# Linear attention and a phase-mixing layer on one core: loading k and v in runs of 5 and 4 tokens, from two queues

## The chip, the core and the metric

One Trainium2 core runs the whole computation in one launch. Its engines each work off their own list of instructions in order: TensorE (matmuls, "PE", weight loads "PEld"), VectorE ("DVE"), ScalarE ("ACT"), GpSimd ("POOL") and SyncE ("SP", which here only issues transfers). Transfers (DMAs) are issued from SyncE, ScalarE and GpSimd, each with its own queue, and are carried by 16 DMA engines. The metric is device time in microseconds; three runs of the kernel before gave 206.93, 206.5 and 206.49 us, with a median of 206.5.

## What is computed

Batch 8, 8 heads of 64 columns, 576 tokens. Linear attention per head, an RMS norm, then a layer that turns each value by an angle and mixes tokens and channels:

```python
kv = np.einsum('bhsd,bhse->bhde', k, v)
out = np.einsum('bhsd,bhde->bhse', q, kv)
x = out / np.sqrt(np.mean(out * out, axis=-1, keepdims=True) + 1e-06) * g_norm   # then heads side by side
theta = x @ w_theta
y = einsum('ts,bsd->btd', w_tok_r, x * cos(theta)) + einsum('ts,bsd->btd', w_tok_i, x * sin(theta))
u = x + y
result = u + np.maximum(u @ w_ch, 0.0)
```

kv sums over all 576 tokens, so it does not matter which token lies on which partition, as long as k and v agree.

## The kernel before

Work is cut into tasks: loads, matmul groups, evacuations, stores. Each has an engine, or a choice of several, and the order in which all tasks are issued is a table of numbers, `TURNS`, played by `play`. A number is a task; a star behind it picks the second of its engines. Entries such as `r9` or `a7` stand for 9 or 7 matmuls of a tile of ones ("fill") with the identity that nobody reads (`idle`); `s2` and `p13` are gates (`hold`): SyncE or GpSimd waits there until the load of that number in the list `landed` has come in.

Per batch b the chain is: load k, v (`loads`), q; **kv** on TensorE (line 301, 4 head pairs, 80 matmuls a batch), copied to `kbd`; q turned by TensorE (line 316) or by a transposing DMA; **raw** = q kv (359); square on ScalarE (381), sums (390), root (GpSimd; for batch 0 ScalarE and VectorE), x (422); x turned to `xT`; **theta** (487) with `wth`; the angle as an integer (503, 509, 513, 519), sine and cosine on ScalarE (526), z (549); **y**, the token mix, with the turned token weights `wT` (572); u into `wn` (577); u turned; **v**, the channel mix (487 again, with `wch`); the sum into `ot` (619), stored (631, 635). The token weights are loaded by GpSimd (`wn`, `wnt`) and turned on TensorE at the start (648, 649); ScalarE changes its function table once from square roots to sines, in the head.

A k or v tile has 128 partitions. Partition p holds tokens 4p to 4p+3 of every head (`heads_in`, line 233: pieces of 1 KB); the last 64 tokens, the **tail**, lie in a column block of their own on partitions 0 to 63 (`tails_in`, line 239: pieces of 256 B), and the same block on partitions 64 to 127 is cleared once (`clear_tails`). kv is five matmul steps j per head: four for the heads' runs, the fifth for the tail. For batch 0 the k loads of either half of the heads are on SyncE's queue, the v loads on ScalarE's, both tails on SyncE's, and kv is split: all of `kvm` (j 0 to 3), then `kvt` (the tail). From batch 1 on, all loads of k and v are on SyncE's queue. Two buffers each (`NKV`) hold k and v, so a load waits for the kv two batches earlier.

Of the kernel before, what the change touches and what calls it, by code (L numbers as in the profile page):

```python
# [17 lines left out]
class Task:  # L18

    def __init__(self, name, engs, fn, deps, takes):  # L20
        self.name, self.engs, self.fn, self.deps, self.takes = name, engs, fn, deps, takes
        self.readers, self.unless = [], []
        self.other, self.at = False, None
# [6 lines left out]
    def run(self):  # L30
        if len(self.engs) == 1:
            self.fn()
        else:
            self.fn(self.engs[int(self.other)])
# [33 lines left out]
r3 a7 r7 r9 6 5 0 2 32 33 1 9 10 r1 a1 4 r2 38 39* 46 3 26 8 47 27 28 29 30 11 12 34 35 36 37 15 7  # L68
54 62 31* 40 41 55* 56 57 14 63* r5 42 43 13 70 71 58 59 44 45 s2 60 123 124* 16 48 49 127 17 72
128 64 65 73 61 50 81 82 66 74 51 52 67 79 80 p13 23 119 24 201 25 68 53 75 95 76 77 120* 89 87 19  # L70
78 200 131 96 69 88* 132* 90 91* 92 85 86 113 97 83 121 122* 21 114 115* 98 107 116 84 93 20 135
94 136* 199 99 100 101 102 103* 125 104 126 108 117 109* 110 129 118 145 137 105 106 111 112 130
22 153 133 18 134 202 203 204 205 206 344 222 154 198 207* 223* 208 138 139 140 146 147 209 210
211 165 224 225 236 215 212 166 237 226 167 229 216* 347 155 141 230 148 156 213 214 142 143 144
157 354 355 168 158 217 149 150 227 228 151 161 493 218 245 219 246* 243 244* 152 220 231 232 233
234 162 368 163 164 196 259 260 261 197 221 253 238 239 369* 235 174 175 240 195 169 170 262 176
254 247 255* 345 241 159 346 491 248 342 249 250 341 256 242 177 171 265 343 361 251 492 271 263
160 264 348 349 362 172 266 189 350 351 252 267* 268 190* 257 277 191 272 273* 258 269 270 274 179
180* 181 352 353 356 487 192 184 182 278 279 280 488 357 358 359 186 185 187 382 303 275 370 371
311 500 299 276 307 304 312 372 373 383 281 282 375 300 360 374 637 308 501 514 309 310 515 313  # L80
314 363 364 389 384 385 376* 494 495 390* 386 365 496 497 634 387 388 391 305 306 498 392* 377 378
379 499 399 400 301 366 367 302 507 508 401 402 380 397 398 381 283 284 502 503 405 188* 639 521
504 406 505 522 285 286 295 296 516 407 408 517 395 396 393 394* 489 173 287 288 289 490 518 506
325 178 646 519 330 290 403 404 409 331* 417 410 411 412 633 657 297 509 510 520 528 327 635 326
636 291 511 769 537 523 298 413* 414 292 293 418 529 419 524 525 420 538 512 513 294 335 336* 328
337 415 638 526 421 640 641 527 422 642 643 765 644 530 423 424 425* 645 535 536 338 551 332 541
647 426 427 416 539 333 428 329* 429 457 531 532 552 648 458 553 540* 542 545 649 546 547* 548 441
430 431 668 442 443 533 534 320 459 432 449 788 460 767 777 334 554 658 659 450 543 557 660 768
650 651 544 563 444 549 451 452 550 558 661 662 652 653 654 655 321 555 564 453 674 315 454 455
456 565 445 316* 559 663 664 556 446 447 448 317 665 656 569 570 764 318 771 481 482* 772 773 571  # L90
774 775 669 483 437 560 438 666 667 566 676 194* 433 434 572 439 319* 670 671 672 484 675* 776 435
# [12 lines left out]
611 840 749 841 842 843 756 940 942 1034 1035 1044 1045 1036 845 844 750 857 858 943 944 1046 1037
945 859 752 753 860 938 754 746 747 1049 861 941 873 757 1047 751* 1048 1060 946 947 966 967 968
846 847 1038 865 866 1050 849 850 851 862 969 951 848 1051 1052 970 1039 1054 939 971 863 864 952
867 868 852 869 870 954 874 955 956 875 953 1040 853 871 872 854 855 856 876 960 961 880 1061* 957
748 1041 1042 962 963 958 1072 1073 1053 1062 959 964 965 988 1055 1056 1057 1066 1067 883 884 885
989 881 877 878 1058 1059 1064 886 990 887 972 973 991 974 975 1004 1063* 1000 984 631* 985 1074*
882 980 981 986 1075 1076 632 1001 982 1002 888* 987 996 997 998 1078 1068* 1003 1065 1007 1077  # L110
983 1069 999 1006 976 992 993 1079 1070 1080* 1081 994 995 977 1082 978 979 1005 1083 1090 1091
1092* 1093 1020 891 1021 1022 1023 1071 889 890 879 1094 1095 1084 1085 1086 892 1087 1014 1008
893 762 1011 1009 763* 1010* 1017 1012 1015 894 1016 1116 1117 1100 1101 1018 1019 1013 1124 1125
1096 1088 1089 1102 1118 1119 1103 1126 1127 1097 1098 1099 1108 1109 1110 1111 1104 1105 1106
1107 1128 1129 1025* 1024* 1139 1112 1113 1114 1130 1131 1132* 1120 1140 1141 1115 1133 1142 1121
# [28 lines left out]
def kernel(  # L144
# [12 lines left out]
    nc = tc.nc  # L157
    B, H, S, D = q.shape
    C = H * D
    P = 128  # L160
# [807 lines left out]
```

## Time and profile before

| what | value |
|---|---|
| median of three runs | 206.5 us |
| the profiled execution | 206.64 us |
| its span, first to last instruction | 204.9 us |
| granted TensorE clock | 0.999 |
| HBM read, written | 33.06 MB, 9.44 MB |
| DMA queue of SyncE (q1) | 52788 packets, 29.17 MB |
| DMA queue of GpSimd (q0) | 15664 packets, 11.49 MB |
| DMA queue of ScalarE (q10) | 1056 packets, 1.05 MB |

The profile is one execution. Busy times overlap between engines; a busy TensorE is not TensorE at its peak, since matmuls are pipelined. A row of instructions names the line, the engine, the operation, and output<-inputs by the program's names; in brackets stands the idle time before it and what ended that. The chain of waits is followed back from the last instruction, at each step to what released it.

### The profile page before, as it was taken

The page shows a single profiled execution, that of the slowest core. Times are in us where ns is not written, and L with a number is a line of the kernel's source. Part 1 is how long each engine was busy: PE and PEld are TensorE (multiplying, and loading weights), DVE is VectorE, ACT ScalarE, POOL GpSimd, SP SyncE. Part 2 cuts the span into 40 slices and gives each one's busy share as a digit, 9 for nine tenths or more (in the row PEclk, how much of TensorE's full clock was granted, in tenths as well). Part 3 has the DMA queues.
Part 4 walks back from the last instruction along what each step waited for, and adds up shares of the span by engine and source line. Part 5 has one row for each costly group of instructions (what it writes and reads, how often), then busy time and mean ns, then how long its engine had stood idle before and what let it go on. Part 6 is the DMA issues. An engine that isn't in the chain of part 4 may idle for free.

```text
span 204.9 us, 5367 instructions
## 1 busy us (share of the span) xinstructions
PE 194.6 (95%) x2137; PEld 136.3 (67%) x2137; DVE 174.8 (85%) x366; ACT 128.3 (63%) x236; POOL 93.2 (45%) x99
## 2 busy tenths in 40 slices
PE   7997798999999999999999999999999999999990
PEld 2475567875778778666866686766866746766850
DVE  6038998898998799999999998998999989897661
ACT  2046998539992989949689678863666670572020
POOL 8310190479146778285673383365664335003013
PEclk9999999999999999999999999999999999999999
DMA  5999999999999999999998929699994545564415
GB/s 189 274 209 202 256 315 188 211 293 297 259 251 233 232 269 258 258 176 180 247 231 253 212 16 241 170 291 287 223 195 128 141 118 146 149 89 141 144 52 182
DMA packets 69532, 42.05 MB, mean 205 GB/s; under 512 B 39828, under 2 KB 65876, under 8 KB 69508
## 3 DMA queue, kind: packets, MB, share of 16 engines
q1 hardware_dynamic: 52788, 29.17, 60.4%
q0 software_dynamic: 15664, 11.49, 33.6%
q10 hardware_dynamic: 1056, 1.05, 1.5%
q8 instruction: 17, 0.28, 0.5%
q14 instruction: 7, 0.06, 0.1%
HBM read 33.06 MB, written 9.44 MB: 207 GB/s over the span
## 4 chain that ended last, share of the span: by engine, by line
PE 69%; DMA 13%; DVE 7%; ACT 5%; issue 2%; SPq 2%; POOL 0%; POOLq 0%; DVEq 0%; ACTq 0%
PE acc L572 29%; PE acc L487 22%; DMA kt<-in_k_dram 13%; PE acc L301 7%; PE tr L316 4%; PE acc L490 3%; PE raw L359 3%; DVE arg L519 2%; DVE x L422 1%; ACT kbd L321 1%; ACT sqb L381 1%; DVE ss L390 1%; SPq L233 1%; ACT arg L509 1%; ACT arg L503 1%
## 5 line engine op out<-in xcount | busy, mean ns | idle before, releaser
L572 PE MATMUL acc<-wT,zm 128*128 128x320 f16 (+1 forms) x512 | 76.7, 286 | 0.0
L400 POOL TENSOR_TENSOR rt<-ss,mhalf 128x8 f32<-128x8 f32 x28 | 47.9, 1714 | 48.1 <-DVE ss L390 48.1
L572 PEld LDWEIGHTS <-zm 128*128 128x128 f16 x512 | 48.2, 98 | 14.7 <-issue 0.9
L526 ACT ACTIVATE sc<-arg 128x1024 f16<-128x1024 int32 x32 | 33.9, 1064 | 10.7 <-DVE arg L519 10.6
L577 DVE SCALAR_TENSOR_TENSOR wn<-acc,gcol,xT 128x320 f16<-128x320 f32 (+1 forms) x64 | 31.4, 510 | 4.8 <-PE acc L572 4.4
L487 PE MATMUL acc<-wth,xT 128*128 128x512 f16 x128 | 31.9, 379 | 0.0
L487 PE MATMUL acc<-wch,wn 128*128 128x512 f16 x128 | 31.8, 379 | 0.1
L503 ACT ACTIVATE arg<-acc 128x512 int32<-128x512 f32 x32 | 19.0, 599 | 10.2 <-PE acc L487 5.0
L519 DVE TENSOR_SCALAR arg<-arg 128x1024 int32<-128x1024 int32 x32 | 23.3, 731 | 1.0 <-ACT arg L509 0.6
L390 DVE TENSOR_REDUCE ss<-sqb 128x8 f32<-128x520 f32 x32 | 21.8, 687 | 1.6 <-ACT sqb L381 1.5
L381 ACT ACTIVATE sqb<-raw 128x512 f32<-128x512 f32 x28 | 16.9, 603 | 8.9 <-PE raw L359 7.1
L301 PE MATMUL acc<-vt,kt 128*64 128x64 f32 x640 | 21.6, 223 | 0.9 <-DMA kt<-in_k_dram 0.9
L549 DVE TENSOR_TENSOR zm<-x,sc 128x1024 f16<-128x1024 f16 x32 | 21.6, 683 | 0.9 <-ACT sc L526 0.8
L301 PEld LDWEIGHTS acc<-vt,kt 128*64 128x64 f32 x640 | 20.3, 138 | 2.2 <-issue 1.8
L631 POOL DMA_DIRECT2D out_dram<-ot x14 | 8.3, 595 | 28.0 <-DVE ot L619 28.0
L422 DVE TENSOR_TENSOR x<-raw,rt 128x512 f16<-128x512 f32 x28 | 19.1, 684 | 1.2 <-POOL rt L400 0.8
L487 PEld LDWEIGHTS <-wn 128*128 128x128 f16 x128 | 12.0, 98 | 11.6 <-issue 0.6
L487 PEld LDWEIGHTS <-xT 128*128 128x128 f16 x128 | 11.8, 98 | 10.9 <-issue 0.2
L572 PE MATMUL acc<-wT,zt 128*128 128x320 f16 (+1 forms) x64 | 18.3, 286 | 0.0
L321 ACT COPY us<-tr 128x512 f16<-128x512 f16 x12 | 6.9, 587 | 13.0 <-PE tr L598 10.8
L400 POOL TENSOR_TENSOR rte<-sse,mhalf 128x4 f32<-128x4 f32 x7 | 9.0, 1284 | 13.0 <-DVE sse L390 13.0
L321 ACT CAST kbd<-acc 64x256 f16<-64x256 f32 (+1 forms) x32 | 11.1, 345 | 6.1 <-PE acc L301 5.6
(101 smaller groups left out, 275.0 us busy)
## 6 DMA issues: line engine op xcount, KB each, us to landing
vt<-in_v_dram SPq DMA_DIRECT2D x7, 1024.0 KB, 9.1
kt<-in_k_dram SPq DMA_DIRECT2D x7, 1024.0 KB, 11.5
out_dram<-ot SPq DMA_DIRECT2D x18, 256.0 KB, 3.2
qh<-in_q_dram POOLq DMA_DIRECT2D x7, 512.0 KB, 9.3
out_dram<-ot POOLq DMA_DIRECT2D x14, 256.0 KB, 3.8
kt<-in_k_dram SPq DMA_DIRECT2D x2, 512.0 KB, 4.7
vt<-in_v_dram ACTq DMA_DIRECT2D x2, 512.0 KB, 8.6
kt<-in_k_dram SPq DMA_DIRECT2D x8, 128.0 KB, 7.8
```

What stands on the lines that cost most here:

```text
L301: nc.tensor.matmul(t[i * D:(i + 1) * D, hp - lo, :], ks, vs, start=(hp == lo and j == 0), stop=(hp == lo + n - 1 and j == NT - 1),)
L321: nc.scalar.copy(out=dst, in_=src)
L390: nc.vector.reduce_sum(out=ss[:], in_=sq_sb.pop((b, j))[:], axis=AXX)
L400: nc.gpsimd.tensor_tensor(out=rt[:], in0=ss[:], in1=mhalf[:, 0:h], op=ALU.pow)
L422: nc.vector.tensor_tensor(out=x_pair[b, p][:, :, a * HC:(a + 1) * HC].rearrange("p t (h e) -> p h t e", e=D), in0=r[:].rearrange("p (h t e ...
L487: nc.tensor.matmul(t[:], piece(kc), w[:, kc, :], start=first, stop=last)
L503: nc.scalar.activation(out=arg[:, 0, :], in_=th_ps[b, j][:], func=AFT.Copy, scale=PER_TURN)
L519: nc.vector.tensor_scalar(out=arg[:], in0=arg[:], scalar1=32 - FINE, scalar2=None, op0=ALU.logical_shift_left)
L526: nc.scalar.activation(out=sc[:], in_=arg_sb.pop((b, j))[:], func=AFT.Sin, bias=0.0, scale=ANGLE,)
L549: nc.vector.tensor_tensor(out=dst, in0=x.unsqueeze(1).broadcast_to((P, 2, w)), in1=sc[:], op=ALU.mult)
L572: nc.tensor.matmul(t[:, 0:hi - lo], s, wT[:, w, lo:hi], start=n == 0, stop=n == len(z) - 1)
L577: nc.vector.scalar_tensor_tensor(out=uTb[b % NUT][:, c, lo:hi], in0=y_ps.pop((b, h, c))[:, 0:hi - lo], scalar=gcol[:, 0:1], in1=xTb[b % NX ...
```

## The change

Partition p of 0 to 63 now holds tokens 5p to 5p+4 (`fives_in`, pieces of 1280 B), partition 64+p holds tokens 320+4p to 320+4p+3 (`fours_in`, pieces of 1 KB). There are no tails; the fifth run's place on partitions 64 to 127 is cleared, now inside each head's columns. All `fives_in` are issued by SyncE, all `fours_in` by ScalarE, for every batch. kv of batch 0 is no longer split into main part and tail. Stores of the last batch may also go to ScalarE's queue (`+` in the table picks a task's third engine).

```diff
-    def heads_in(eng, dst, src, b, hs):
+    def heads_of(t):
+        return t[:].rearrange("p (h e) -> p h e", h=H)
+
+    def fives_in(eng, dst, src, b, hs):
         eng.dma_start(
-            out=rows_of(dst)[:, hs, :],
-            in_=src[b, hs, 0:SM, :].rearrange("h (p j) d -> p h (j d)", j=NJ),
+            out=heads_of(dst)[0:TL, hs, :],
+            in_=src[b, hs, 0:TL * NT, :].rearrange("h (p j) d -> p h (j d)", j=NT),
         )
-    def tails_in(eng, dst, src, b, hs):
+    def fours_in(eng, dst, src, b, hs):
         eng.dma_start(
-            out=tails_of(dst)[0:TL, hs, :],
-            in_=src[b, hs, SM:S, :].rearrange("h s d -> s h d"),
+            out=heads_of(dst)[TL:P, hs, 0:NJ * D],
+            in_=src[b, hs, TL * NT:S, :].rearrange("h (p j) d -> p h (j d)", j=NJ),
         )
...
-            nc.vector.memset(t[TL:P, H * NJ * D:H * NT * D], 0.0)
+            nc.vector.memset(heads_of(t)[TL:P, :, NJ * D:NT * D], 0.0)
...
+    def parts_in(n, t, src, b, hs, w, old):
+        return [add(f"load {n}{b}A{w}", "SP", lambda: fives_in(nc.sync, t, src, b, hs), old),
+                add(f"load {n}{b}B{w}", "ACT", lambda: fours_in(nc.scalar, t, src, b, hs), old)]
...
         for n, t, src in (("k", kt, k), ("v", vt, v)):
-            t = t[b % NKV]
-            k_ += [add(f"load {n}{b}", "SP",
-                       lambda t=t, src=src: heads_in(nc.sync, t, src, b, all8), old),
-                   add(f"load {n}{b}e", "SP",
-                       lambda t=t, src=src: tails_in(nc.sync, t, src, b, all8), old)]
+            k_ += parts_in(n, t[b % NKV], src, b, all8, "", old)
...
-            fin.readers = [add(f"st{w} {b} {j}{hh}", "SP|POOL",
+            fin.readers = [add(f"st{w} {b} {j}{hh}", "SP|POOL|ACT" if split else "SP|POOL",
...
-r3 a7 r7 r9 6 5 0 2 32 33 1 9 10 r1 a1 4 r2 38 39* 46 3 26 8 47 27 28 29 30 11 12 34 35 36 37 15 7
-54 62 31* 40 41 55* 56 57 14 63* r5 42 43 13 70 71 58 59 44 45 s2 60 123 124* 16 48 49 127 17 72
+r9 3 r8 r1 2 0 19 12 8 1 28 6 7 29 30* 31* a5 5 36 37 44 45* 4 32 33 46 34 35* 9 52 10 53* 60 38
+47 48 39 40 61 54 55 56 11 68 69 r3 41 42 43 49 62 63 16 21 57 58 17 117 118 121 122 50 59 70 71
+s10 13 14 125 126 64 65 77 78 72 51 73 76 66 22 74 75 129 79 80* 15 87 88 89 85 67 86* 23 93 130*
```

The whole table is new. The idle matmuls in it: before r3 a7 r7 r9, r1 a1 r2 and r5, 35 in all, 26 of them ahead of the first kv; now r9 r8 r1, a5 and r3, 26 in all, 18 ahead of the first kv. The gates: before, SyncE waits for batch 0's k tail (`s2`) and GpSimd for the tail of the real token weights (`p13`); now SyncE waits for the imaginary token weights (`s10`, `wn_86`) and GpSimd for the real ones (`p12`). The first list below is SyncE's order at the start of the program (kt_64 and vt_66 are batch 0's tiles, kt_65 and vt_67 batch 1's; sqe is the place of g_norm), before:

```order
L233 DMA kt_64<-in_k_dram 128x4x256 x2
L239 DMA kt_64<-in_k_dram 64x8x64
L275 DMA sqe_97<-in_g_norm_dram 1x64
L239 DMA vt_66<-in_v_dram 64x8x64
L676 DMA gate_100<-kt_64 1x1
L239 DMA kt_65<-in_k_dram 64x8x64
L239 DMA vt_67<-in_v_dram 64x8x64
L233 DMA vt_67<-in_v_dram 128x8x256
L233 DMA kt_65<-in_k_dram 128x8x256
```

and now:

```order
L230 DMA vt_66<-in_v_dram 64x4x320
L230 DMA kt_64<-in_k_dram 64x4x320
L272 DMA sqe_97<-in_g_norm_dram 1x64
L230 DMA vt_66<-in_v_dram 64x4x320
L230 DMA kt_64<-in_k_dram 64x4x320
L670 DMA gate_101<-wn_86 1x1
L230 DMA vt_67<-in_v_dram 64x8x320
L230 DMA kt_65<-in_k_dram 64x8x320
```

The tails are gone from both sides of the gate, and the gate reads another load. ScalarE's list in the head, between the first and the second change of its function table, before (sqb, sqe: squares; rs, rse: roots; wT: turned token weights; arg: angles):

```order
L381 ACTIVATE sqe_98<-acc_200 128x4x64
L455 ACTIVATE xT_82<-tr_194,gcol 128x4x128
L409 ACTIVATE rs_334<-ss_323 128x8
L409 ACTIVATE rs_338<-ss_330 128x8
L455 ACTIVATE xT_82<-tr_187,gcol 128x4x128
L409 ACTIVATE rse_359<-sse_332 128x4
L413 ACT_TABLE_LOAD
L413 ACTIVATE warm<-quarter 128x1
L503 ACTIVATE arg_384<-acc_182 128x512
```

and now:

```order
L403 ACTIVATE rs_329<-ss_327 128x8
L449 ACTIVATE xT_82<-tr_189,gcol 128x4x128
L403 ACTIVATE rse_340<-sse_336 128x4
L407 ACT_TABLE_LOAD
L407 ACTIVATE warm<-quarter 128x1
L497 ACTIVATE arg_365<-acc_182 128x512
L503 ACTIVATE arg_365<-acc_182 128x512
L236 DMA vt_67<-in_v_dram 64x8x256
L497 ACTIVATE arg_391<-acc_225 128x512
L497 ACTIVATE arge_399<-acc_155 128x256
```

A load of batch 1's v now stands between the angles of batch 0's theta; 17 more of its 18 loads stand elsewhere in ScalarE's list. In all, SyncE's loads of k, v and g_norm go from 33 to 19. The end of GpSimd's list held the last batch's stores, before:

```order
L635 DMA out_dram<-ote_1313 64x256
L631 DMA out_dram<-ot_755 128x512
L635 DMA out_dram<-ote_875 64x256 x2
L631 DMA out_dram<-ot_755 128x512
L631 DMA out_dram<-ot_881 128x512
L635 DMA out_dram<-ote_1313 64x256 x2
```

and now ScalarE's list ends with two of them, while GpSimd's ends with one `ote` store:

```order
L520 ACTIVATE sc_401<-arg_365 128x1024
L315 COPY us_703<-tr_196 128x512
L315 COPY us_705<-tr_189 128x512
L625 DMA out_dram<-ot_747 128x512
L629 DMA out_dram<-ote_1575 64x256
```

The last `ote` tile's two halves are stored from two queues, and the copy of the last turned u (`use`), the last thing ScalarE did before, is now VectorE's.

More of the change, by code (lines that the diff above doesn't have):

```diff
@@ L22, in __init__ @@
         self.readers, self.unless = [], []
-        self.other, self.at = False, None
+        self.other, self.at = 0, None
     def free_at(self):
@@ L33, in run @@
         else:
-            self.fn(self.engs[int(self.other)])
+            self.fn(self.engs[self.other])
 class Slots:
@@ L124, in play @@
     for turn in turns:
-        if turn.endswith("*"):
-            tasks[int(turn[:-1])].other = True
+        if turn[-1] in "*+":
+            tasks[int(turn[:-1])].other = "*+".index(turn[-1]) + 1
     for at, turn in enumerate(turns):
@@ L628, in store @@
         ot = ot_sb[b, j]
-        queue = nc.gpsimd if e == "POOL" else nc.sync
+        queue = {"SP": nc.sync, "POOL": nc.gpsimd, "ACT": nc.scalar}[e]
         if full(j):
@@ L693 @@
     got, q_got, k_got = {}, {}, {}
-    def halves_of_0(eng, e, t, src, n):
-        a = [add(f"load {n}0a", e, lambda: heads_in(eng, t, src, 0, lo4)),
-             add(f"load {n}0e", "SP", lambda: tails_in(nc.sync, t, src, 0, all8))]
-        return [a[0], add(f"load {n}0b", e, lambda: heads_in(eng, t, src, 0, hi4)), a[1]]
-    k0, v0 = halves_of_0(nc.sync, "SP", kt[0], k, "k"), halves_of_0(nc.scalar, "ACT", vt[0], v, "v")
-    for hp in range(NHP):
-        k_got[0, hp, "m"] = [k0[hp // 2], v0[hp // 2]]
-        k_got[0, hp, "t"] = [k0[2], v0[2]]
+    def parts_in(n, t, src, b, hs, w, old):
+        return [add(f"load {n}{b}A{w}", "SP", lambda: fives_in(nc.sync, t, src, b, hs), old),
+                add(f"load {n}{b}B{w}", "ACT", lambda: fours_in(nc.scalar, t, src, b, hs), old)]
+    for w, hs in (("a", lo4), ("b", hi4)):
+        both = parts_in("k", kt[0], k, 0, hs, w, []) + parts_in("v", vt[0], v, 0, hs, w, [])
+        for hp in range(hs.start // 2, hs.stop // 2):
+            k_got[0, hp] = both
     q_got[0, 0] = [add("load q0a", "POOL", lambda: q_in(0, lo4))]
@@ L745 @@
             first = prev = None
-            for js, m in ((range(NJ), "m"), (range(NJ, NT), "t")) if b == 0 else ((range(NT), ""),):
-                for hp in range(lo, lo + n):
-                    got_k = k_got[b, hp, m] if m else k_got[b, hp]
-                    t = add(f"kv{m} {b} {hp}", "PE",
-                            lambda b=b, hp=hp, lo=lo, n=n, js=js: kv_piece(b, hp, lo, n, js),
-                            [*got_k, prev], [] if prev else [PS_ACC])
-                    first, prev = first or t, t
+            for hp in range(lo, lo + n):
+                t = add(f"kv {b} {hp}", "PE", lambda b=b, hp=hp, lo=lo, n=n: kv_piece(b, hp, lo, n),
+                        [*k_got[b, hp], prev], [] if prev else [PS_ACC])
+                first, prev = first or t, t
             outs = [add(f"ko{n} {b} {i}", "ACT|DVE",
```

113 lines of the change are left out of this document (51 added, 62 removed), and 3 rows, old and new, of the table TURNS.

## The prediction

> **What bounds the kernel now.** I read the page first: busy shares, then the chain that ended last.
>
> ```profile
> PE 194.6 (95%) x2137; PEld 136.3 (67%) x2137; DVE 174.8 (85%) x366; ACT 128.3 (63%) x236; POOL 93.2 (45%) x99
> PE 69%; DMA 13%; DVE 7%; ACT 5%; issue 2%; SPq 2%; POOL 0%; POOLq 0%; DVEq 0%; ACTq 0%
> ```
>
> TensorE is busy 95% of the span and carries 69% of the chain; one transfer into kt carries 13%. To see where, I asked for the busy time by stretches (columns: stretch, then busy us and count of PE, PEld, DVE, ACT, POOL, the granted clock, DMA share, GB/s).
>
> ```profile
> 2.00:5.00 3.00, 3.00 (x9) 1.06 (x7) 2.60 (x6) 0.22 (x2) 3.00 (x6) 1.00 0.93 306
> 7.00:10.00 3.00, 3.00 (x27) 1.42 (x26) 0.00 (x0) 0.00 (x0) 0.00 (x0) 1.00 1.21 250
> 10.00:12.00 2.00, 2.00 (x38) 1.42 (x32) 0.05 (x1) 0.00 (x0) 0.54 (x1) 1.00 1.44 212
> 23.00:29.00 6.00, 5.90 (x53) 3.62 (x52) 5.96 (x14) 5.75 (x10) 4.18 (x7) 1.00 1.12 333
> 90.00:120.00 30.00, 29.53 (x333) 20.66 (x333) 29.16 (x58) 23.06 (x40) 18.11 (x14) 1.00 1.06 202
> sum 168.00, PE 166.91 PEld 119.71 DVE 153.83 ACT 110.11 POOL 79.28; mean PE 33.38 PEld 23.94 DVE 30.77 ACT 22.02 POOL 15.86
> ```
>
> The sum row is over 32 to 200 us: TensorE is busy 166.91 of 168. So from 32 us on there is almost nothing to take away, and a gain has to come from the head, up to the first matmul of batch 1's kv, or from the tail. The head is two things: TensorE matmuls on ones ("fill") that do no work, and waits on loads. The DMA engines are loaded throughout (share about 1 or more), and the pace falls from 306 GB/s, when only the 1 KB pieces of k and v run, to 250 and 212 GB/s once the 256 B tails and q's pieces mix in.
>
> ```profile
> 9.56 1.15 PE L301 MATMUL acc<-vt,kt 128*64 128x64 f32 x32
> 12.09 1.57 PE L301 MATMUL acc<-vt,kt 128*64 128x64 f32 x40
> 13.79 0.45 PE L301 MATMUL acc<-vt,kt 128*64 128x64 f32 x8
> 15.61 1.24 PE L658 MATMUL raw<-fill,ident 128*128 128x512 f16 x5
> 17.99 0.41 PE L648 MATMUL tr<-ident,wn 128*128 128x128 f16 x4 [1.03 <-DMA wn<-in_moe_w_tok_i_dram]
> 21.91 1.90 PE L487 MATMUL acc<-wth,xT 128*128 128x512 f16 x8
> 32.33 2.55 PE L301 MATMUL acc<-vt,kt 128*64 128x64 f32 x80 [0.90 <-DMA kt<-in_k_dram]
> 14.07 18.12 DMA kt<-in_k_dram
> 3.22 0.63 SPq L239 DMA_DIRECT2D vt<-in_v_dram  x1
> vt<-in_v_dram SPq DMA_DIRECT2D x1, 128.0 KB, 9.8
> ```
>
> These are TensorE's milestones in the head (start, length), a piece of the chain of waits, and the v tail's issue with its time to landing. Batch 0's kv ends at 14.24 us: the v tail, issued at 3.22, lands 9.8 us later, at 13.0. The token weights hold TensorE until 17.99, theta starts at 21.91, and batch 1's kv waits 0.90 us for a k that was issued at 14.07 and took 18.12 us.
>
> **The change, part by part.** *No tails.* Each k or v of a batch was 1024 pieces of 1 KB and 512 of 256 B; it becomes 512 of 1280 B and 512 of 1 KB. Bytes are the same; 16 x 512 = 8192 of the page's 69532 packets go.
>
> ```profile
> DMA packets 69532, 42.05 MB, mean 205 GB/s; under 512 B 39828, under 2 KB 65876, under 8 KB 69508
> kt<-in_k_dram SPq DMA_DIRECT2D x7, 1024.0 KB, 11.5
> kt<-in_k_dram SPq DMA_DIRECT2D x8, 128.0 KB, 7.8
> kt<-in_k_dram SPq DMA_DIRECT2D x2, 512.0 KB, 4.7
> vt<-in_v_dram ACTq DMA_DIRECT2D x2, 512.0 KB, 8.6
> ```
>
> A tail of 128 KB takes 7.8 us to land (last column, median), against 11.5 for eight times the bytes. Batch 0 needs 2.36 MB of k and v. At 306 GB/s from 2 us that would be 9.7 us; with q's pieces sharing from about 6 us I take 10.3, against 13.0 now. TensorE arrives there sooner too: the table's idle matmuls drop from 35 to 26. Five of them took 1.24 us, of which the last one's 0.38 us pipeline is no issue time, so 0.215 us each; the eight fewer ahead of the first kv are 1.7 us (9.56 becomes 7.85), and all nine 1.9 us. From 7.85, the first half (1.57 us for 40, as in the row at 12.09), five idle matmuls (1.1), q's turn (0.4) and the second half (1.57) end near 12.4, 1.8 us sooner than 14.24.
>
> That gain meets the next late thing: the loads on GpSimd's queue, which are not changed in size.
>
> ```profile
> 4.93 0.61 POOL L261 DMA_DIRECT2D wn<-in_moe_w_tok_i_dram  x1
> wn<-in_moe_w_tok_i_dram POOLq DMA_DIRECT2D x1, 576.0 KB, 13.0
> 5.47 0.81 POOL L269 DMA_DIRECT2D wth<-in_moe_w_theta_dram  x1
> wth<-in_moe_w_theta_dram POOLq DMA_DIRECT2D x1, 512.0 KB, 15.7
> 22.27 1.28 ACT L413 ACT_TABLE_LOAD   x1
> ```
>
> The imaginary token weights land at 4.93 + 13.0 = 17.9, theta's at 5.47 + 15.7 = 21.2. With k and v gone from the DMA engines some two microseconds sooner, shared with q, I take 17.0 for the first. But the SyncE gate has moved: it now holds batch 1's loads until those weights land, and then lets loads of 0.66 MB each go, with 0.52 MB each from ScalarE's queue beside them, just when theta's weights come. Before, the small tails stood at the head of that queue and kept the big loads away until about 23 us, where the pace rises to 333 GB/s. So theta's weights may land anywhere from 20.2 (their lead kept) to 23.7 (0.8 MB of the released loads at 333 GB/s ahead of them); I take 22.5 and theta's start at 22.7. From theta's start to a ready batch 1 took 32.33 - 0.90 - 21.91 = 9.5 us, with ScalarE busy 5.75 of 6.00 us: that stretch is ScalarE's chain. In it stands the 1.28 us table load, which in the new order comes after square roots that are done before theta; against it stands one DMA issue (0.49, below). 22.7 + 9.5 - 1.3 + 0.5 = 31.4; one more group of token weight transposes, 0.4 us long, stands ahead of theta now and no longer in this stretch. So batch 1's kv starts near 31.0 in place of 32.33. Batch 1's loads have no tails in front and none of the 7.42 us issue below, so the 0.90 us wait goes. **Head: -1.4 us**, from -2.9 (weights as early as TensorE) to +1.0 (later still).
>
> *ScalarE issues half of the loads.* 18 loads in place of 2 and two stores.
>
> ```profile
> 1.57 0.98 ACTq L233 DMA_DIRECT2D vt<-in_v_dram  x2
> 14.07 7.42 SPq L233 DMA_DIRECT2D kt<-in_k_dram  x1
> 67.55 0.60 ACT sqb L381
> 87.01 0.50 ACT arg L509
> 90.84 0.38 PE raw L359 x4
> ```
>
> Two issues took 0.98 us, 0.49 each. The chain leaves TensorE between 67.3 and 90.8 us and runs through ScalarE and VectorE; the two ACT rows are the first and the last of 15 ScalarE pieces there, with about 7 of the 24 us. The 12 issues after the head lie between 32 and about 150 us, so by their share 12 x 24/118 = 2.4 of them fall there: 2.4 x 0.49 x 7/24 = 0.35 us. Elsewhere ScalarE has room (23.06 of 30 us busy in 90 to 120) and TensorE sets the pace. In the new order three evacuations also pass from ScalarE to VectorE, which has 0.84 of 30 us left in 90 to 120; I add 0.05 and let the bounds cover the rest. What waits behind an issue on ScalarE is its queue of squares and sines; if an issue blocked as SyncE's did (7.42 us, behind some 2000 pieces of its own queue), all of them would. Each queue now holds 512 pieces a load, and a load stands well behind the kv that frees its buffer, so I take no blocking. **Middle: +0.4**, from -1.0 (another order can also fit better) to +3.
>
> *The tail.*
>
> ```profile
> 199.51 0.69 DVE L619 SCALAR_TENSOR_TENSOR ot<-acc,us 128x512 f32<-128x512 f32 x1
> 200.68 0.28 issue
> 200.96 0.54 POOL out_dram L635
> 201.50 0.52 POOLq L963
> L323 DVE COPY use<-tr 128x256 f16<-128x256 f16 x5 | 1.4, 280 | 0.0
> ```
>
> The last two stores are issued one after the other on GpSimd; now one goes to ScalarE's queue: -0.53. But the last small copy moves from ScalarE to VectorE, behind the 0.69 us finish: +0.28. **Tail: -0.25.**
>
> *Hidden.* The 14 loads taken from SyncE's queue and the stores shifted between SyncE and GpSimd: neither engine is in the chain after 14 us except at the end. The transposes behind them on SyncE can only come sooner. If that cover went, a late transpose would hold TensorE by what it is late. The cleared columns are the same four memsets.
>
> Sum: -1.4 + 0.4 - 0.25 = -1.25. The profiled execution took 206.64 us (204.9 span and 1.7 around it), 0.14 over the median of 206.5. From the median, 206.5 - 1.25: **205.3 us**.
>
> **Rivals.** *Half-height loads are slow (slower).* Every load of k and v now writes 64 partitions. If such a load moves at half the pace, 306 becomes 153 GB/s: 2.36 MB end at 17.4 us and batch 0's kv near 19.0, 4.7 us after today's 14.24; today's wait for token weights (1.03) and the idle matmuls behind kv (1.24) cover 2.3 of that: about +2.4 us, **209 us**. It decides where k and v land after today's last tail, below 2.36 MB / (13.0 - 2) = 215 GB/s for both queues together. For it: ScalarE's two loads of 512 KB landed in 8.6 us where SyncE's equal ones took 4.7, so two queues filled at one time were served one after the other, and then only one half of the partitions is written at a time. Against it: the DMA share of 1.21 from 7 to 10 us shows several queues in flight at once, and the 64-partition tails' slowness may be their 256 B pieces as well as their height. Chance 0.2.
>
> [...] No row of this profile separates height from piece size.
>
> *The gain is hidden anyway.* If theta's weights come at 23.7 us, batch 1's kv starts 1.2 us later than I take it, at 32.2: the head gains 0.1, and 206.5 - 0.1 + 0.4 - 0.25 = **206.55**, no change. For it: the wait on token weights shows that GpSimd's loads pace the head already. Chance 0.17.
>
> *More of it comes through.* Weights are not delayed and the middle costs nothing: -2.9 - 0.25, **203.3 us**. For it: GpSimd's loads lose their slow company from 7 to 23 us. Chance 0.18.
>
> **How the numbers follow.** My forecast, 204.2 to 206.1, has 0.45; the larger gain 0.18, no change 0.17, slower 0.2. A measurement of this kernel tells about 0.2%, 0.4 us. Faster by more than that: 0.45 + 0.18 = 0.63; within it 0.17; slower 0.2. The range leaves out the lower end of the larger gain (under 203.0, half of the 0.18) and the upper part of the slow rival (over 207.8, half of the 0.2): **203.0 to 207.8**.
>
> **What would show it.** Batch 1's kv (80 matmuls at once) starting near 31 us with no DMA wait; theta near 22.7; batch 0's kv over by 12.5; ScalarE issues of about 0.5 us and none over 1; the last two stores side by side. I am wrong if batch 0's kv waits on vt or kt past 12 us, if the chain passes through more transfers, or if TensorE's busy time from 32 us on falls below 99% of it.

## The result, and the profile after

The changed kernel takes **219.0 us** (median of 4 runs, 217.2 to 221.8) against 206.7 us for the kernel before, measured with it (206.5 to 207.0): ratio **1.055, 95% interval 1.050 to 1.060**. Here and below a ratio leaves out runs over 1.5% above the fastest of their kernel (here the one of 221.8 us), while a median is over all runs. By the ratio the change costs some 11 us where I had forecast 1.25 us less. The profiled execution took 217.96 us, with a span of 215.8 us.

First the page of the changed kernel: busy time by engine, the shares of the chain that ended last, and the DMA packets.

```profile
PE 194.6 (90%) x2128; PEld 136.9 (63%) x2128; DVE 175.4 (81%) x372; ACT 127.9 (59%) x230; POOL 92.6 (43%) x97
DMA 32%; PE 24%; issue 17%; DVE 12%; POOL 8%; ACT 5%; ACTq 0%; POOLq 0%; DVEq 0%
DMA packets 61404, 42.04 MB, mean 195 GB/s; under 512 B 31668, under 2 KB 58100, under 8 KB 61380
```

TensorE has the same 194.6 us of work; its share fell from 95 to 90% because it waits. The chain went from 13% transfers to 32%. There are 8128 packets fewer, close to the 8192 that the change promised. The mean of 195 GB/s against 205 says no more than that the same bytes are spread over a longer span.

Then the busy time by stretches (stretch; busy us of PE, PEld, DVE, ACT, POOL; granted clock, DMA share, GB/s).

```profile
2.00:5.00 3.00, 3.00 (x9) 1.06 (x7) 2.60 (x6) 0.23 (x2) 3.00 (x6) 1.00 0.91 213
32.00:211.00 179.00, 168.13 (x1880) 120.58 (x1880) 155.03 (x318) 112.19 (x198) 81.33 (x74) 1.00 0.99 189
```

The first row is the one to hold against its twin in the prediction. From 2 to 5 us the DMA engines are as busy as before (0.91, before 0.93), with almost nothing but k and v to move, and they move 213 GB/s where they moved 306. The second row says that the loss is not in the head alone: from 32 us to the end of TensorE's work 11 of 179 us are idle, where before 1 of 168 was.

Where TensorE waits in the changed kernel (what it waited for: us in all, times, the longest), and the head's milestones on it:

```profile
PE acc L295 <- DMA kt<-in_k_dram: 4.6, 2, 2.7
PE acc L295 <- DVE zm L543: 2.5, 2, 1.6
PE acc L295 <- DMA vt<-in_v_dram: 2.3, 1, 2.3
PE raw L353 <- DMA qD<-qh: 1.8, 1, 1.8
```

```profile
10.90 2.40 PE L295 MATMUL acc<-vt,kt 128*64 128x64 f32 x40 [2.65 <-DMA kt<-in_k_dram]
15.16 1.39 PE L295 MATMUL acc<-vt,kt 128*64 128x64 f32 x40
23.65 1.03 PE L481 MATMUL acc<-wth,xT 128*128 128x512 f16 x4
35.23 2.55 PE L295 MATMUL acc<-vt,kt 128*64 128x64 f32 x80 [2.33 <-DMA vt<-in_v_dram]
```

kv (line 295) waits for k or v in batch 0, in batch 1 and again further on. Batch 0's kv ends at 15.16 + 1.39 = 16.55 us (before 14.24), theta starts at 23.65 (21.91), batch 1's kv at 35.23 (32.33). The first 40 products also take 2.40 us where the next 40 take 1.39; that is a matter of the granted clock, 0.50 from 11 to 13.3 us (last section). Three transfers in the chain of waits (start, length):

```profile
24.72 10.38 DMA vt<-in_v_dram
50.87 21.47 DMA kt<-in_k_dram x2
79.69 16.20 DMA qD<-qh
```

And three rows of the list of DMA issues (KB each, median us from issue to landing):

```profile
vt<-in_v_dram SPq DMA_DIRECT2D x7, 640.0 KB, 9.0
kt<-in_k_dram SPq DMA_DIRECT2D x7, 640.0 KB, 11.4
qD<-qh SPq DMA_TRANSPOSE x8, 8.0
```

A load of 640 KB takes as long to land as 1 MB did (9.0 and 11.4 us against 9.1 and 11.5 before), with 512 KB more on the other queue in 9.6 and 9.7. The transposes of q behind them take 8.0 us, where they took 6.4.

To place the loss I split each span at two starts of TensorE's k/v products, batch 1's and the last batch's. The same three stretches serve for the experiments. Each row is from the one profiled execution of its kernel, in us:

| kernel | to batch 1's kv | from there to the last kv | from there to the end | span |
|---|---|---|---|---|
| before | 32.3 | 111.1 | 61.5 | 204.9 |
| after | 35.2 | 118.1 | 62.5 | 215.8 |
| old layout, new order (t2; t2b) | 32.0; 32.8 | 108.7; 110.5 | 62.2; 62.3 | 202.9; 205.6 |
| even and odd partitions (t1) | 34.1 | 112.7 | 62.3 | 209.1 |
| fives on 32 to 95 (t5) | 36.3 | 110.8 | 62.2 | 209.3 |
| half height in the old order (t3, its run of 215.5 us) | 34.3 | 118.0 | 61.4 | 213.7 |
| one queue (t6) | 39.6 | 125.8 | 62.2 | 227.6 |

Of the 10.9 us between the two profiled spans, 2.9 are in the head, 7.0 in the middle, 1.0 at the end.

### The profile page after: what moved, and what is told of

It reads as the page before. It is cut to its first block, busy times and chain, and to the rows that moved or that the text cites. A ratio compares the mean times of both kernels' runs of the same rounds, so it can differ in the third digit from the quotient of the medians.

```text
span 215.8 us, 5367 instructions
## 1 busy us (share of the span) xinstructions
PE 194.6 (90%) x2128; PEld 136.9 (63%) x2128; DVE 175.4 (81%) x372; ACT 127.9 (59%) x230; POOL 92.6 (43%) x97
## 4 chain that ended last, share of the span: by engine, by line
DMA 32%; PE 24%; issue 17%; DVE 12%; POOL 8%; ACT 5%; ACTq 0%; POOLq 0%; DVEq 0%
DMA kt<-in_k_dram 14%; PE acc L566 8%; DMA qD<-qh 8%; PE acc L481 6%; POOL rt L394 5%; PE acc L295 5%; DMA vt<-in_v_dram 5%; DVE ss L384 3%; DMA xD<-x 3%; DMA out_dram<-ot 2%; DVE wn L571 2%; POOL out_dram L625 2%; PE tr L310 2%; DVE x L416 2%; PE raw L353 1%
## 5 line engine op out<-in xcount | busy, mean ns | idle before, releaser
L566 PEld LDWEIGHTS <-zm 128*128 128x128 f16 x512 | 48.6, 98 | 15.4 <-issue 0.2
L481 PE MATMUL acc<-wth,xT 128*128 128x512 f16 x128 | 32.7, 379 | 0.6 <-DVE xT L451 0.4
L295 PE MATMUL acc<-vt,kt 128*64 128x64 f32 x640 | 22.3, 229 | 9.6 <-DMA kt<-in_k_dram 4.6
L295 PEld LDWEIGHTS acc<-vt,kt 128*64 128x64 f32 x640 | 21.1, 143 | 11.4 <-issue 3.1
L513 DVE TENSOR_SCALAR arg<-arg 128x1024 int32<-128x1024 int32 x32 | 22.8, 721 | 0.7 <-ACT arg L503 0.4
L625 POOL DMA_DIRECT2D out_dram<-ot x18 | 10.4, 576 | 24.7 <-DVE ot L613 19.4
L481 PEld LDWEIGHTS <-wn 128*128 128x128 f16 x128 | 11.9, 98 | 12.4 <-issue 1.4
L613 DVE SCALAR_TENSOR_TENSOR ot<-acc,us 128x512 f32<-128x512 f32 x20 | 13.5, 684 | 2.6 <-PE acc L481 2.0
L315 ACT CAST kbd<-acc 64x256 f16<-64x256 f32 (+1 forms) x28 | 10.1, 359 | 9.3 <-PE acc L295 9.0
L315 ACT COPY qD<-tr 128x512 f16<-128x512 f16 x9 | 5.2, 589 | 16.1 <-PE tr L310 15.3
## 6 DMA issues: line engine op xcount, KB each, us to landing
kt<-in_k_dram SPq DMA_DIRECT2D x7, 640.0 KB, 11.4
```

Source lines behind the costliest of these rows:

```text
L295: nc.tensor.matmul(t[i * D:(i + 1) * D, hp - lo, :], ks, vs, start=(hp == lo and j == 0), stop=(hp == lo + n - 1 and j == NT - 1),)
L481: nc.tensor.matmul(t[:], piece(kc), w[:, kc, :], start=first, stop=last)
L513: nc.vector.tensor_scalar(out=arg[:], in0=arg[:], scalar1=32 - FINE, scalar2=None, op0=ALU.logical_shift_left)
L566: nc.tensor.matmul(t[:, 0:hi - lo], s, wT[:, w, lo:hi], start=n == 0, stop=n == len(z) - 1)
```

## The experiments

Theories. **Height**: a transfer that writes only partitions 0 to 63, or only 64 to 127, moves at a lower pace, and two of them at once do not make it good. Rivals: the **new order** of issue; the **second queue** or ScalarE's issue time; the **size of the pieces**.

**The layout moved to even and odd partitions (t1).** Pieces, queues and order of the changed kernel:

```diff
-            out=heads_of(dst)[0:TL, hs, :],
+            out=heads_of(dst)[0:P:2, hs, :],
-            out=heads_of(dst)[TL:P, hs, 0:NJ * D],
+            out=heads_of(dst)[1:P:2, hs, 0:NJ * D],
-            nc.vector.memset(heads_of(t)[TL:P, :, NJ * D:NT * D], 0.0)
+            nc.vector.memset(heads_of(t)[:, :, NJ * D:NT * D], 0.0)
```

> The changed kernel with one edit: the runs of 5 tokens go to the even partitions (0, 2, ..., 126) and the runs of 4 to the odd ones, so that each transfer reaches over all 128 partitions and still fills 64. Pieces, bytes, queues and order of issue are those of the changed kernel; only the two clears of zeros cover all partitions, and the first of them stands ahead of the first loads. If half-height transfers are slow because they reach only one half of the partitions: the 640 KB loads fall from 9.0 and 11.4 us to about 6 to 9, the 1280 B packets from a mean of 93 ns to about 60, the first k/v product no longer waits past 10 us, and the time is 204 to 208 us. If 64 rows are slow wherever they lie: 217 to 221. If the new order of issue is the cause: 217 to 221. If ScalarE's queue or its issue time is the cause: 217 to 221.

Measured: 209.6 us, ratio 1.011 (1.003 to 1.020). Nine of the eleven lost us come back with nothing changed but which 64 partitions a load fills; order, second queue and piece size are the same, so none of them made those nine. The loads in it (list of DMA issues):

```profile
vt<-in_v_dram SPq DMA_DIRECT2D x7, 640.0 KB, 6.0
kt<-in_k_dram SPq DMA_DIRECT2D x7, 640.0 KB, 8.2
```

They fell into the range that the height theory gave, but the time missed it (204 to 208). The first loads were issued 1.2 us later, behind the clears, and TensorE's first wait for k grew to 4.7 us.

**The layout of before in the new order (t2, and once more as t2b).** Part A is the 1 KB runs on all 128 partitions on SyncE's queue, part B the tail on ScalarE's:

```diff
-            out=heads_of(dst)[0:TL, hs, :],
-            in_=src[b, hs, 0:TL * NT, :].rearrange("h (p j) d -> p h (j d)", j=NT),
+            out=rows_of(dst)[:, hs, :],
+            in_=src[b, hs, 0:SM, :].rearrange("h (p j) d -> p h (j d)", j=NJ),
-            out=heads_of(dst)[TL:P, hs, 0:NJ * D],
-            in_=src[b, hs, TL * NT:S, :].rearrange("h (p j) d -> p h (j d)", j=NJ),
+            out=tails_of(dst)[0:TL, hs, :],
+            in_=src[b, hs, SM:S, :].rearrange("h s d -> s h d"),
```

> The changed kernel's order of issue and its two queues with the layout of before: part A of each load is the 128 partitions with runs of 4 tokens on SyncE's queue, part B the 64-token tail in 256 B pieces on ScalarE's queue. If the half-height layout is the cause, the new order does no harm without it: 204 to 208 us, and k and v of batch 3 no longer hold TensorE near 70 us. If the new order (or the transfers' place in it) is the cause: 214 to 220. If ScalarE's queue as such is the cause: 212 to 220, since it still carries a fifth of the bytes and as many transfers.

> The run with the old layout in the new order once more, for its interval (it gave 206.44 us, 0.994 to 1.001 of before). If order, second queue and tail are worth what I predicted of them without the head's gain (some 0.2 us): 206.2 to 207.0. If they are worth the whole sum that I predicted: 205.3 to 205.8.

Measured: 206.4 us, ratio 0.997 (0.994 to 1.001), and 206.3 us, ratio 0.994 (0.990 to 0.998). The whole loss is gone with the layout. The new order with its second queue is no slower than the old one, by the second run a little faster. Its stretches row for 32 us to the end of TensorE's work shows no idle time worth the name:

```profile
32.00:198.00 166.00, 165.69 (x1871) 120.16 (x1873) 153.06 (x314) 110.60 (x197) 81.85 (x74) 1.00 0.90 201
```

**Half height in the old order (t3).** The kernel before, with the new layout for batches 1, 3, 5 and 7 only, both loads on SyncE's queue:

```diff
-                       lambda t=t, src=src: heads_in(nc.sync, t, src, b, all8), old),
+                       lambda t=t, src=src: (fives_in if b % NKV else heads_in)(nc.sync, t, src, b, all8), old),
-                       lambda t=t, src=src: tails_in(nc.sync, t, src, b, all8), old)]
+                       lambda t=t, src=src: (fours_in if b % NKV else tails_in)(nc.sync, t, src, b, all8), old)]
```

> The kernel before, its order and its one queue, with the half-height layout for batches 1, 3, 5 and 7 only (fives on 0 to 63 and fours on 64 to 127, both on SyncE's queue); batches 0, 2, 4 and 6 are read as before. If half-height transfers are slow whatever the order: slower than before by a good part of the change's loss, 209 to 214 us, and within the one run the fives of 640 KB take as long to land as the 1 MB loads, though they are 0.62 of their bytes. If the new order or the second queue is the cause: 205 to 207, within 0.5% of before, since neither is in this kernel.

Measured: one run of 212.1 us at a granted clock of 0.999, and three of 215.5, 217.2 and 217.7 us at 0.962 to 0.976; the kernel before, measured with them, took 206.5 to 208.8 us at 0.991 to 1.000. Only the first can be held against it. It is 5 us slower, within the 209 to 214 of the height theory and outside the 205 to 207 of the rivals: half height costs time in the old order and on one queue too, though here on the word of one run. The trace is that of the run of 215.5 us, so part of what it lost is its lower clock. Its longest wait on TensorE's timeline (start, length, group, idle time before):

```profile
65.33 0.61 PE L336 MATMUL tr<-ident,qh 128*128 128x128 f16 x4 [3.36 <-DMA qh<-in_q_dram]
65.73 3.41 PE L592 MATMUL acc<-wT,zm 128*128 128x320 f16 x12
```

And the stretch behind it:

```profile
66.00:72.00 6.00, 6.00 (x31) 3.84 (x30) 0.07 (x1) 1.04 (x2) 0.93 (x1) 0.56 1.08 177
```

Not a load of k or v is late here but one of q, on GpSimd's queue, which shares the 16 DMA engines with SyncE's, where the fives of 640 KB took 11.5 and 13.2 us: in this trace the packets of GpSimd's queue took 32% of those engines' time and SyncE's 66%. In the 6 us behind the wait the granted clock is 0.56, by my estimate worth 6 x 0.44 = 2.6 us. But the clock of this run is also low from 18 to 27 us (0.62), with no wait longer than 1.3 us in front of it, so the trace does not show how much of the run's time the height cost.

**The transfers by themselves (t4, t4b).** No computation; each kind runs alone, twice.

> Nothing is computed: each kind of transfer is run by itself, twice, with a full stop between them (the output is not the reference's). Kinds: the 1 MB load on 128 partitions; fives alone on 0 to 63 (640 KB); fours alone on 64 to 127 (512 KB, ScalarE's queue); fives and fours at once on the two queues; the same on SyncE's queue alone; fives alone on even partitions; fives on even with fours on odd on two queues; the 128 KB tail; load and tail; the 1 MB load split over the two queues. If the height sets the pace: low and high alone move at about 200 GB/s (640 KB in 3 to 4 us behind the fixed time), even alone near the whole's pace, the two halves at once between one half's pace and the whole's. If the two halves at once on two queues reach the pace of the whole, the half-height layout as such costs nothing and the loss in the kernel must come from the order in which the two queues are served. If the piece of 1280 B is slow by itself, even is as slow as low.

> Nothing is computed; transfers by themselves again, twice each, with a full stop between them (the output is not the reference's): the 1 MB load on 128 partitions; fives on 0 to 63; fives on 32 to 95; a quarter (256 KB on 0 to 31); the two quarters 0 to 31 and 96 to 127 at once; fives on 32 to 95 with both quarters on the other queue; fives on even partitions; two loads of fives on 0 to 63 behind one another; two on 32 to 95. If the halves of the partitions are what shares a limit: 32 to 95 takes 4.4 us as the even ones did, 0 to 63 5.6; two behind one another take about 9.2 on 0 to 63 and 6.9 on 32 to 95; the quarter takes about 2 + 256 KB / 180 KB per us = 3.4. If the pace goes by the number of neighbouring partitions: 32 to 95 is as slow as 0 to 63.

From the list of DMA issues of the first kernel (KB, us from issue to landing): "low" is fives on 0 to 63, "pair" fives and fours at once on two queues, "pairq" the same on one, "even" and "evenodd" the layout of t1, "wholetail" the load of before.

```profile
whole<-in_k_dram SPq DMA_DIRECT2D x1, 1024.0 KB, 5.7
low<-in_k_dram SPq DMA_DIRECT2D x1, 640.0 KB, 5.6
even<-in_k_dram SPq DMA_DIRECT2D x1, 640.0 KB, 4.4
pair<-in_k_dram ACTq DMA_DIRECT2D x1, 512.0 KB, 7.6
pairq<-in_k_dram SPq DMA_DIRECT2D x1, 512.0 KB, 7.3
evenodd<-in_k_dram ACTq DMA_DIRECT2D x1, 512.0 KB, 6.1
wholetail<-in_k_dram SPq DMA_DIRECT2D x1, 128.0 KB, 5.8
```

640 KB on 0 to 63 take as long as 1 MB on all partitions. Counted from the first issue, one k or v of a batch is complete in 6.3 us as before the change (its tail is issued 0.45 us behind the load), in 7.6 as the change loads it, in 6.1 on even and odd partitions. The pace once data flow is in the stretches (last column GB/s, two columns before it the clock; no TensorE work in this kernel): whole; low in its first half microsecond, and behind that; pair, twice; evenodd; wholetail.

```profile
6.25:7.50 1.25, 0.82 (x1) 0.00 (x0) 1.00 1.09 387
33.00:33.50 0.50, 0.00 (x0) 0.00 (x0) 1.00 1.11 389
33.50:34.75 1.25, 0.00 (x0) 0.00 (x0) 1.00 1.13 213
50.50:51.50 1.00, 0.00 (x0) 0.00 (x0) 1.00 1.11 214
52.50:53.25 0.75, 0.00 (x0) 0.00 (x0) 1.00 1.13 217
79.25:81.00 1.75, 0.00 (x0) 0.00 (x0) 1.00 1.08 390
93.50:95.00 1.50, 0.00 (x0) 0.00 (x0) 1.00 1.09 389
```

One half alone begins at the whole's pace, 389 GB/s for half a microsecond (why was not looked into), and then moves at 213, a little over half of the whole's 387. Even and odd partitions together move at 390, load and tail at 389. The DMA engines' share is 1.08 to 1.13 in every row: it says that they are held, not that they move data.

Both halves issued at once show 214 and 217, no more than one. But they hardly ran together: by the packets in the trace the fives, issued at 47.2 us, moved from 48.6 to 52.2 us and the fours from 50.9 to 54.2. In the changed kernel, packets of both do run together for a part of the time. Three stretches of it, the first with fives and fours, the second with fives alone, the third with fours and almost nothing else:

```profile
26.00:28.00 2.00, 2.00 (x26) 1.44 (x24) 2.00 (x4) 1.45 (x3) 2.00 (x3) 1.00 1.09 346
42.00:47.00 5.00, 5.00 (x56) 4.29 (x54) 4.15 (x10) 1.82 (x4) 3.82 (x4) 1.00 1.12 202
51.00:53.00 2.00, 2.00 (x20) 1.10 (x19) 1.95 (x4) 1.41 (x5) 2.00 (x4) 1.00 1.15 207
```

So what is slow is the time in which only one half is written, 202 and 207 GB/s; with both it is 346. In half-microsecond steps up to 160 us, fives and fours both moved in 15.5 us and only one of them in about 70: two queues did not bring the halves together often. Why a load of the second queue mostly follows that of the first stays open.

Fives on 32 to 95, a quarter from each half, in the second kernel:

```profile
low<-in_k_dram SPq DMA_DIRECT2D x1, 640.0 KB, 5.9
band<-in_k_dram SPq DMA_DIRECT2D x1, 640.0 KB, 4.6
even<-in_k_dram SPq DMA_DIRECT2D x1, 640.0 KB, 4.5
```

So here neither the 1280 B piece nor 64 neighbouring partitions were slow (4.6 us on 32 to 95), only the transfer that stays within one half (5.9). Two loads of fives behind one another landed in the median 5.9 us after issue on 0 to 63 and 4.5 on 32 to 95, as if alone: their issues were 2.7 us apart, so the 9.2 and 6.9 that I expected were not seen. The quarter alone (256 KB on 0 to 31), by my estimate 3.4 us, took 3.0.

**The same band in the kernel (t5).** Fives on 32 to 95, the fours in two loads on 0 to 31 and 96 to 127:

```diff
-            out=heads_of(dst)[0:TL, hs, :],
+            out=heads_of(dst)[P // 4:P - P // 4, hs, :],
-        eng.dma_start(
-            out=heads_of(dst)[TL:P, hs, 0:NJ * D],
...
+        for p, at in ((0, TL * NT), (P - P // 4, TL * NT + P // 4 * NJ)):
+            eng.dma_start(
+                out=heads_of(dst)[p:p + P // 4, hs, 0:NJ * D],
+                in_=src[b, hs, at:at + P // 4 * NJ, :].rearrange("h (p j) d -> p h (j d)", j=NJ),
```

> The changed kernel with the runs of 5 tokens on partitions 32 to 95 and the runs of 4 on 0 to 31 and 96 to 127 (two loads of 256 KB behind one another on ScalarE's queue in place of one of 512 KB). Still 64 partitions in one piece for the fives, so the clears stay small and the first loads wait for nothing. If what counts is which partitions a transfer reaches (0 to 63 is one half; 32 to 95 takes a quarter from each half, and alternate partitions did well in the kernel with even and odd): the 640 KB loads come down from 9.0 and 11.4 us to 6 to 9, the fours stay slow, and the time is between that kernel's and the changed one's, 210 to 215 us. If any 64 neighbouring partitions are slow: 218 to 223, with two more issues of 0.6 us for each batch on ScalarE.

Measured: 214.0 us (four runs, 211.4 to 215.6), ratio 1.026 (1.021 to 1.030), as the height theory had it, although ScalarE issues two loads in place of one for each k and v. The v fives land in 6.9 us; the k fives, in 10.8, did not come into the 6 to 9 expected. The middle is as short as before (110.8); the head is the longest but one in the table, with a first wait for k of 5.0 us, which was not followed further.

**One queue (t6).** The fours issued by SyncE:

```diff
-                add(f"load {n}{b}B{w}", "ACT", lambda: fours_in(nc.scalar, t, src, b, hs), old)]
+                add(f"load {n}{b}B{w}", "SP", lambda: fours_in(nc.sync, t, src, b, hs), old)]
```

> The changed kernel with the fours issued by SyncE instead of ScalarE, all else alike. If the height is the cause and the queue has no part: 217 to 222. If ScalarE's queue (or the mixing of two queues' pieces on the 16 engines) made the loss: 206 to 212. If SyncE's queue becomes the worse place, since its transposes and stores then stand behind all of k and v: 221 to 226.

Measured: 229.7 us, ratio 1.108 (1.105 to 1.111), worse than the worst that I gave. The second queue did not make the loss, it held it down: by the packets, fives and fours both moved in 8.0 us, against 15.5 with two queues. TensorE's longest waits there:

```profile
PE acc L295 <- DMA vt<-in_v_dram: 7.9, 1, 7.9
PE acc L295 <- DMA kt<-in_k_dram: 6.9, 2, 3.5
```

**Full-height first, even and odd later (t8).** Batch 0 in the layout of before, batches 1 to 7 as in t1; GpSimd clears the first tiles for the new layout behind batch 0's copies:

```diff
+        if b == 0 and lo and i:
+            for x in (vt[0], kt[0]):
+                nc.gpsimd.memset(heads_of(x)[:, :, NJ * D:NT * D], 0.0)
```

> The changed kernel's order and queues; batch 0 in the layout of before (128 partitions and a tail), batches 1 to 7 with the fives on even and the fours on odd partitions. GpSimd clears the first tiles for their new layout behind batch 0's copies, so no first load waits for a clear. The kernel with even and odd partitions for every batch took 209.6 us, 3.2 over the same order with the old layout. If that rest was its late first loads (1.2 us later, and what followed in the head): 206 to 207.3 here. If 64 partitions cost time in the steady part even where they reach both halves: 208 to 210, and the products of batches 2 to 4 start later than with the old layout (50.9, 64.4, 79.2).

Measured: 212.9 us, ratio 1.027 (1.022 to 1.032), for a reason of my own making. The clears (here on GpSimd's timeline) waited for batch 0's kv, and q's loads stood behind them in GpSimd's list:

```profile
14.06 0.52 POOL L334 MEMSET vt<- 128x512 f32 x1 [11.11 <-PE acc L321]
14.52 0.53 POOL L334 MEMSET kt<- 128x512 f32 x1
14.99 0.76 POOL L267 DMA_DIRECT2D qh<-in_q_dram  x1
```

TensorE waited 5.1 us for q, and batch 1's kv started at 38.4. The time therefore doesn't answer the question; the middle stretch does in part: 109.9 us against 108.7 and 110.5 with the old layout, so loads of 64 partitions from both halves need not cost time there. What t1 itself has over t2 and t2b is 1.3 to 2.1 us in the head and 2.2 to 4.0 in the middle, where TensorE waited 2.5 us for q and the clock fell behind that wait; whether its late start brought this on is not shown.

**Two attempts on the head (t9, t10).** Both start from t2. In t9 batch 0's k goes wholly by SyncE's queue and its v by ScalarE's; in t10 the tails' products of batch 0 stand behind the others of two head pairs:

```diff
+        first = (nc.sync, "SP") if n == "k" or b else (nc.scalar, "ACT")
+        second = (nc.scalar, "ACT") if n == "v" or b else (nc.sync, "SP")
```

```diff
+        pieces = [(hp, j) for j in range(NJ if b == 0 else NT)]
+        if b == 0 and last:
+            pieces += [(x, NJ) for x in range(lo, lo + n)]
```

> The changed kernel's order with the layout of before (128 partitions and a 64-token tail), as in the run with the old layout, and for batch 0 alone k wholly on SyncE's queue and v wholly on ScalarE's, so that no queue carries all four 512 KB loads. If the head is what still waits there (k/v of batch 0 stood 1.1 us twice, the second time to 13.7): 204.5 to 206, and the first product of batch 1 starts near 31. If those waits are covered by what comes behind (the token weights' landing): 206 to 207, as with the old layout.

> The run with the old layout in the new order, with one edit on TensorE: in batch 0 the tails' products of two head pairs stand behind both pairs' other products, as in the kernel before, so the first pair no longer waits 1.1 us for the tail's 64 KB. If that wait is on the path: 205.2 to 206.2 us. If the second half of batch 0, which lands at 13.7, sets the head anyway: 206 to 206.8, like the run with the old layout.

t9: 210.1 us, ratio 1.014 (1.009 to 1.018), a miss; v on ScalarE's queue landed in 10.8 us where it took 5.7 on SyncE's in t2, and kv waited 3.6 us for it. t10: 206.5 us, ratio 0.996 (0.993 to 1.000), no different from t2. The wait for the first half's tail shrank from 1.09 to 0.72 us, and the one for the second half grew from 1.09 to 1.40: the second half of batch 0 sets the head, not the tail. No version here clearly beats t2.

**TensorE kept busy in the wait (t12).** The changed kernel with 12 more products of constants ahead of the first kv (`r1` becomes `r13`).

> The changed kernel with 12 more products of constants on TensorE ahead of batch 0's first k/v product (216 ns each, 2.6 us), so that TensorE is busy while it waits for k. In the changed kernel it stood idle from 8.25 to 10.90 us and the 40 products behind took 2.40 us at a granted clock of 0.50, where the next 40 took 1.39. If the idle time is what brought the clock down: the first 40 take about 1.4 us, all of batch 0's k/v is about 1 us earlier, and the time is 0.5 to 1.2 us below the changed kernel's 217 to 220. If the clock there has another cause (the start, the work itself): 40 products in 2.4 us again, and no change.

Measured: 220.3 us, ratio 1.063 (1.053 to 1.072), not below the changed kernel. But the 40 products took 1.39 us, and the stretch stood at clock 1.00:

```profile
11.76 1.39 PE L295 MATMUL acc<-vt,kt 128*64 128x64 f32 x40 [2.02 <-DMA kt<-in_k_dram]
15.12 1.39 PE L295 MATMUL acc<-vt,kt 128*64 128x64 f32 x40 [0.34 <-DMA kt<-in_k_dram]
```

So with less idle time, 2.02 in place of 2.65 us, the clock stayed up as expected; this is one execution of each, and the last section has a longer wait that left the clock alone. The microsecond was not gained: the first k came 0.86 us later here (11.76 against 10.90) and TensorE waited 0.34 us for the second half's k, so that the second half starts at 15.12 where it had started at 15.16.

## Why the prediction was wrong

- **The step that failed: the pace.** "Batch 0 needs 2.36 MB of k and v. At 306 GB/s from 2 us that would be 9.7 us." I took a pace that 128-partition loads had shown for loads of half the height. The same stretch shows 213 GB/s; by itself, a half in full flow moves at 213 where the whole moves at 387, and two halves issued at once mostly follow one another (t4). The case was in the prediction as the rival "Half-height loads are slow", with a chance of 0.2. Its half pace, 153 GB/s, was my assumption, which no row of the profile before shows; the runs showed 213 in its place. Of its two reasons against, the DMA share of 1.21 was no evidence, since the share is 1.13 at 213 GB/s and 1.09 at 387. The slowness of the tails was no evidence either: by itself a tail landed in 2.7 us (t4), so neither its pieces nor its height made the 7.8 to 9.8 us in the kernel.
- **The head.** Forecast -1.4, measured +2.9 us at batch 1's kv (35.23 against 32.33); the rival's +2.4 was near by luck, since it had batch 0's kv end at 19.0 and half of that delay covered behind it. TensorE was there at 8.25 (forecast 7.85) and waited 2.65 us for k. Batch 0's kv ended at 16.55, not 12.4; theta started at 23.65, not 22.7; the 0.90 us wait at batch 1 did not go, it became 2.33.
- **The middle.** Forecast +0.4 with bounds of -1 and +3, measured +7.0. Here both forecast and rival failed: I priced half height in the head alone and took the 14 later loads as hidden, because TensorE was busy 166.91 of 168 us. That row says that nothing can be gained there; it does not say how much later a load may come. The wait of 0.90 us for batch 1's k had shown that one of them came just in time. In the changed kernel TensorE stood idle five times in the middle, 7.4 us in all: for k (1.91), a transposed q (1.81), q (1.18), and twice for VectorE's z (1.64 and 0.82), where what held VectorE was not followed.
- **"The transposes behind them on SyncE can only come sooner"**: wrong. They took 8.0 us to land in place of 6.4, and TensorE waited 1.8 us for one.
- **ScalarE's issues**: right in kind. They took 0.60 us (forecast 0.49) and none over 0.83; none blocked. The list of its loads in the changed kernel's trace has 602 ns as the median and 832 as the longest.
- **The tail**: from the last product to the end of the span 4.54 us against 4.71 (200.15 to 204.86 before, 211.29 to 215.83 after), -0.17 where I forecast -0.25. The last stretch as a whole is 0.7 to 1.0 us longer in every kernel of the table with the new order, t2 with them; I had not looked at the products' order there, and what makes it so was not tried.
- **The packets saved**: 8128 fewer bought nothing that can be seen. Load and tail together move at 389 GB/s and are complete in 6.3 and 5.9 us (two times in t4), the two long pieces on even and odd partitions at 390 and in 6.1 and 5.9.
- **What was right outside the layout.** t2 keeps order, queue and tail of the change: 0.997 and 0.994 of before, some 0.6 to 1.3 us, near the -1.25 of my sum by chance: the sum had it in the head, and there batch 1's kv starts at 32.0 and 32.8 us, not near 31.0; the middle is 108.7 and 110.5 us long against 111.1, where I had expected +0.4.

## What to carry to other kernels

Give a transfer partitions of both halves, 0 to 63 and 64 to 127: here 640 KB landed in 4.4 to 4.6 us on 32 to 95 or on every second partition, in 5.6 to 5.9 on 0 to 63. Do not count on a second load for the other half: the two moved fast only while their packets ran together (346 GB/s, against 202 and 207 for one half alone), and mostly they did not, even from two queues (15.5 us against about 70). Longer pieces did not make up for it: 1280 B pieces on one half moved at 213 GB/s, 1 KB pieces on all partitions at 387. Loads that hide behind a busy engine still have a slack, and it belongs in the sum: TensorE was busy 166.91 of 168 us, and the middle still grew by 7.0 us. An engine busy all the time bounds what can be gained, not what can be lost.

## What the runs showed of the hardware

*Half height.* A half in full flow moved at 213 GB/s by itself (t4) and at 202 and 207 in the changed kernel, the whole at 387 (t4). With both halves issued at once t4 shows 214 and 217, though their packets hardly ran together; from 26 to 28 us of the changed kernel, with packets of both halves running together, it was 346. Fives on 32 to 95 and on the even partitions landed in 4.4 to 4.6 us, on 0 to 63 in 5.6 to 5.9 (t4, t4b). What in the chip ties the pace to the halves was not shown.

*A wait can be paid twice.* After an idle time of 2.65 us TensorE's granted clock was 0.50 over the stretch from 11 to 13.3 us in the changed kernel, and 40 products took 2.40 us in place of 1.39. The longest such wait is one of 7.9 us with one queue (t6). The rows are the stretch with it and the one behind it, at 0.50:

```profile
58.00:66.00 8.00, 0.50 (x6) 0.21 (x3) 3.30 (x7) 2.33 (x4) 1.02 (x1) 0.74 1.29 211
66.00:71.00 5.00, 4.58 (x84) 4.54 (x84) 0.01 (x1) 0.00 (x0) 0.00 (x0) 0.50 0.90 113
```

The clock was low behind shorter ones too: 2.47 us in t1 (0.50 from 60 to 62 us) and 1.8 us in t12 (0.58 from 72.7 to 76.8 us). But 2.33 and 1.91 us in the changed kernel left it at 1.00 (35 to 38 and 72 to 76 us), and so, by the 1.39 us of the 40 products behind it, did a longer wait in t9:

```profile
11.57 1.39 PE L301 MATMUL acc<-vt,kt 128*64 128x64 f32 x40 [3.60 <-DMA vt<-in_v_dram]
```

The length of the gap alone doesn't decide it; what does was not shown.
